# Two small opening loads change queue: c on GpSimd's, x tile 0 on SyncE's, in a kernel that keeps TensorE busy all the time

## The chip, the core and the metric

The kernel runs on one core of one Trainium2 chip. The metric is the device time of one execution in microseconds (us).

## The reference, cut to what matters

A vector c gives six modulation vectors. A block of layer norm, modulation and grouped-query attention follows (2048 queries and keys, 32 query heads on 8 key heads of width 128), then a gated MLP.

```python
mod = (_silu(c) @ w_mod).reshape(c.shape[0], 6, 1, -1)      # c: 1x512, w_mod: 512x3072
sa, ca, ga, sb, cb, gb = ...
h = _layernorm(x) * (1 + ca) + sa                             # x: 2048x512
x = x + ga * attention(h, k_cache, v_cache, wq, wo)
h = _layernorm(x) * (1 + cb) + sb
x = x + gb * gated_mlp(h, ...)
```

The first query projection needs `ca` and `sa`, which need silu(c) and the first two 512-column parts of `w_mod`. It also needs the first 128 rows of x (tile 0), normalised.

## The kernel before

Only the opening matters here: all loads that are wanted in the first 9 us, the work on c, and TensorE's program order up to the first attention scores. In these traces VectorE and the matmuls of TensorE keep the order in which the program emits them (in c_pool_warm_13_3, below, VectorE starts on a tile 3.6 us after it landed, because other work stood first), so this order is part of the argument.

```python
# loads. nc.scalar, nc.sync, nc.gpsimd name the engine whose queue takes the transfer
nc.scalar.dma_start(out=c_bf[:], in_=c_dram)                       # 1 KB
nc.scalar.dma_start(out=x_sb[:, 0, :], in_=x_dram[:, 0, :])         # tile 0, 128 KB
for i in range(2):
    part = slice(i * D, (i + 1) * D)
    nc.sync.dma_start(out=wmod_a[:, :, part], in_=wmod_dram[:, :, part])   # 512 KB each
# ... then on nc.sync: wq in two parts, k, x tile 1, k, x tiles 2 and 3, k transposed, v ...

# VectorE (nc.vector) and ScalarE (nc.scalar): silu of c
nc.vector.memset(zeros[:], 0.0)
nc.vector.memset(ones_bf[:], 1.0)
nc.vector.tensor_copy(out=c_f[:], in_=c_bf[:])
nc.scalar.activation(out=en[:], in_=c_f[:], func=ACT.Exp, scale=-1.0)
# ... on nc.vector: en + 1, sig = 1 / en, sc = c_f * sig
nc.vector.tensor_copy(out=sc_bf[:], in_=sc[:])

def warm(n):                       # n matmuls of zeros, 512 columns each
    ...

def mod_part(i, wmod, w0, mc_ps):  # 16 matmuls of one column
    for dt in range(NDT):
        for kt in range(NDT):
            nc.tensor.matmul(mc_ps[:, i * NDT + dt : i * NDT + dt + 1],
                lhsT=wmod[:, kt, w0 + dt * P : w0 + (dt + 1) * P],
                rhs=sc_bf[:, kt : kt + 1], ...)

# statistics of tile 0: bn_stats, bn_aggr on nc.vector, rstd on nc.gpsimd, normalise on nc.vector
xns0 = ln1_norm(0, 1, ln1_stats(0, 1))

warm(10)
mod_part(0, wmod_a, 0, mc_ps)      # wants part 0 of wmod_a, and sc_bf
warm(6)
mod_part(1, wmod_a, D, mc_ps)      # wants part 1
# ... four transposes of xn of tile 0, the query projection, the first scores (QK)
```

Of the kernel before, what the change touches and what calls it, by code (L numbers as in the profile page):

```python
# [575 lines left out]
def kernel(  # L576
# [19 lines left out]
    nc = tc.nc  # L596
# [21 lines left out]
    x_dram = A_x[0].rearrange("(t p) d -> p t d", p=P)  # L618
# [8 lines left out]
    c_dram = c[0].rearrange("(p j) -> p j", p=P)  # L627
# [19 lines left out]
    x_sb = res.tile([P, NT, D], BF16, name="x_sb")  # L647
# [46 lines left out]


    c_bf = res.tile([P, NDT], BF16, name="c_bf")
    nc.scalar.dma_start(out=c_bf[:], in_=c_dram)
    nc.scalar.dma_start(out=x_sb[:, 0, :], in_=x_dram[:, 0, :])
    for i in range(2):
        part = slice(i * D, (i + 1) * D)  # L700
        nc.sync.dma_start(out=wmod_a[:, :, part], in_=wmod_dram[:, :, part])
    k_nat = early.tile([P, SK], BF16, name="kT")

    def load_k_nat(half):
# [190 lines left out]
    for k in range(2):  # L895
        for dt in (2 * k, 2 * k + 1):
# [3 lines left out]
            else:  # L900
                nc.scalar.activation(
                    out=dst,
                    in_=src,
# [17 lines left out]
    for hf, copy in enumerate((nc.vector.tensor_copy, nc.scalar.copy)):  # L921
        copy(
            out=qTs[0][:, 2 * hf : 2 * hf + 2, 0:P],
            in_=q_ps[hf][:, 0 : 2 * P].rearrange("p (h q) -> p h q", h=2),
# [377 lines left out]
    for f in range(NFT):  # L1302
# [6 lines left out]
        out=ok1[:], in0=rall[:], scalar1=1.0 / SAFE, scalar2=None, op0=ALU.is_ge  # L1309
# [8 lines left out]
        out=bad[:], in0=okm[:], scalar1=-1.0, scalar2=1.0, op0=ALU.mult, op1=ALU.add  # L1318
# [137 lines left out]
```

## Time and profile before

| what | before | where from |
|---|---|---|
| time, median of six runs | 1321.10 us (1320.93 to 1321.20) | the runs |
| span of the profiled execution | 1319.7 us | the page |
| TensorE busy | 1312.4 us | the page |
| first modulation matmul | 5.42 us | timeline |
| second modulation, first matmul | 7.81 us | timeline |
| first scores (QK) matmul | 10.86 us | timeline |

TensorE does some 1300 us of matmuls with hardly a gap, so a delay of the first scores is a delay of the end.

From the view of the tile wmod_a in before, the time of its two transfers from issue to landing:

```profile
DMA to landing us min/median/max: 4.5/5.0/5.6
```

Six matmuls of zeros took 2.08 us; the cold rate, which the first ten show, is 0.43 us each, the warm rate 0.22 us. The landings: part 0 at 0.73 + 4.5 = 5.2 us, part 1 at 1.48 + 5.6 = 7.1 us.

### The profile page before, as it was taken

What the parts mean: (1) busy time and instruction counts of PE and PEld (TensorE: products, weight loads), DVE (VectorE), ACT (ScalarE), POOL (GpSimd) and SP (SyncE); (2) the same over time, 40 slices, a digit from 0 to 9 for tenths busy, and PEclk for the clock granted to TensorE, in tenths of its full rate; (3) what the DMA queues carried; (4) which work ended last, traced back from release to release, by engine and by line L of the source; (5) the groups of instructions that cost most, each with busy time, mean ns of one, the idle gap of its engine ahead of it and who ended that gap; (6) DMA issues with size and microseconds to landing.
All of it is one profiled execution on the core that took longest, in us unless ns stands there. A gap on an engine that the chain in (4) does not pass through costs nothing.

```text
span 1319.7 us, 27930 instructions
## 1 busy us (share of the span) xinstructions
PE 1312.4 (99%) x12359; PEld 858.6 (65%) x12359; DVE 470.7 (36%) x1162; ACT 1077.1 (82%) x1061; POOL 51.4 (4%) x96
## 2 busy tenths in 40 slices
PE   9999999999999999999999999999999999999998
PEld 5666666666666666666666666666666666644445
DVE  5622222222222222222222222222222566794444
ACT  7899999999999999999999999999999999650000
POOL 1201000000000000000000000000000000020000
PEclk9999999999999999999999999999999999999999
DMA  6542121112101111211110211121111112144300
GB/s 180 146 99 46 21 45 37 37 17 50 37 17 37 30 37 37 33 33 38 33 38 13 53 38 33 17 53 22 33 13 21 25 31 32 34 114 81 70 20 26
DMA packets 148944, 58.64 MB, mean 44 GB/s; under 512 B 138480, under 2 KB 144880, under 8 KB 148816
## 3 DMA queue, kind: packets, MB, share of 16 engines
q1 hardware_dynamic: 141792, 37.65, 15.4%
q0 software_dynamic: 4432, 16.91, 4.5%
q10 hardware_dynamic: 2592, 2.23, 0.5%
q8 instruction: 98, 1.61, 0.5%
q14 instruction: 30, 0.25, 0.1%
HBM read 21.89 MB, written 2.10 MB: 18 GB/s over the span
## 4 chain that ended last, share of the span: by engine, by line
PE 99%; DVE 0%; ACT 0%; issue 0%; DVEq 0%
PE o_ps L995 35%; PE s_ps L973 33%; PE misc L1027 8%; PE misc L940 8%; PE misc L1336 7%; PE s_ps L1182 2%; PE s_ps L1221 2%; PE o_ps L1357 1%; PE o_ps L781 1%; PE s_ps L1357 1%; PE misc L850 0%; DVE hT L809 0%; PE misc L1344 0%; ACT pT L980 0%; DVE tmp L1369 0%; DVE yout L1370 0%
## 5 line engine op out<-in xcount | busy, mean ns | idle before, releaser
L980 ACT ACTIVATE pT<-s_ps 128x1024 bf16<-128x1024 f32 x1024 | 1043.8, 1024 | 82.0 <-PE s_ps L973 6.7
L995 PEld LDWEIGHTS <-pT 128*128 128x128 bf16 x8192 | 548.5, 98 | 241.2
L995 PE MATMUL o_ps<-v,pT 128*128 128x129 bf16 x8192 | 631.5, 220 | 0.0
L973 PE MATMUL s_ps<-qT,kT 128*128 128x512 bf16 x2048 | 608.9, 379 | 0.3 <-ACT pT L980 0.2
L1006 DVE RECIPROCAL rall<-o_ps 128x2 f32<-128x2 f32 x256 | 43.5, 170 | 744.5 <-PE o_ps L995 741.1
L973 PEld LDWEIGHTS <-kT 128*128 128x128 bf16 x2048 | 199.3, 98 | 119.2 <-issue 0.8
L1027 PE MATMUL misc<-wo_g,oT 128*128 128x512 bf16 x512 | 194.1, 379 | 0.0
L940 PE MATMUL misc<-hT,wq_g 128*128 128x512 bf16 (+2 forms) x528 | 190.7, 371 | 0.1
L1007 DVE TENSOR_TENSOR onorm<-o_ps,rall 128x256 bf16<-128x256 f32 x256 | 108.6, 424 | 8.8
L1336 PE MATMUL misc<-wsp,z 128*128 128x512 bf16 (+2 forms) x560 | 100.7, 336 | 0.0
L951 DVE CAST qT<-misc 128x512 bf16<-128x512 f32 x127 | 86.2, 679 | 2.0 <-PE misc L940 2.0
L1336 PEld LDWEIGHTS <-z 128*128 128x128 bf16 x560 | 50.6, 98 | 48.5
L1040 DVE TENSOR_TENSOR xacc<-misc,xacc 128x512 f32<-128x512 f32 x112 | 76.0, 678 | 0.0
L940 PEld LDWEIGHTS <-wq_g 128*128 128x128 bf16 x528 | 50.4, 98 | 1.2 <-issue 0.4
L1027 PEld LDWEIGHTS <-oT 128*128 128x128 bf16 x512 | 50.1, 98 | 0.8
L1351 DVE TENSOR_TENSOR gb<-misc,bsp_bc 128x512 bf16<-128x512 f32 (+1 forms) x28 | 18.4, 658 | 58.9 <-PE misc L1336 58.9
L1182 PE MATMUL s_ps<-win_sb,hT 128*128 128x448 bf16 x128 | 27.0, 352 | 0.0
L1192 ACT ACTIVATE z<-s_ps 128x896 bf16<-128x896 f32 x16 | 14.7, 917 | 14.9 <-PE s_ps L1182 14.9
L1221 PE MATMUL s_ps<-hT,win_sb 128*128 128x512 bf16 x112 | 24.5, 379 | 0.0
L1229 ACT ACTIVATE z1T<-s_ps 128x1024 bf16<-128x1024 f32 x14 | 14.3, 1023 | 10.1 <-PE s_ps L1221 9.1
L692 DVE BATCH_NORM_STATS2 bnst<-x_sb 128x6 f32<-128x512 bf16 x32 | 21.8, 683 | 1.3 <-DMA x_sb<-in_A_x_dram 0.8
L1357 PE MATMUL o_ps<-wout_sb,yT 128*128 128x512 bf16 x84 | 20.1, 379 | 0.0
(88 smaller groups left out, 269.6 us busy)
## 6 DMA issues: line engine op xcount, KB each, us to landing
wq_g<-in_A_wq_dram POOLq DMA_DIRECT2D x7, 512.0 KB, 3.8
v<-in_A_v_cache_dram POOLq DMA_DIRECT2D x7, 512.0 KB, 6.0
wo_g<-in_A_wo_dram POOLq DMA_DIRECT2D x7, 512.0 KB, 4.7
oT<-onorm SPq DMA_TRANSPOSE x128, 2.4
wsp<-in_w_mod_dram POOLq DMA_DIRECT2D x1, 2048.0 KB, 9.0
out_dram<-yout ACTq DMA_DIRECT2D x16, 128.0 KB, 1.7
win_sb<-in_B_w_in_dram POOLq DMA_DIRECT2D x1, 1792.0 KB, 7.8
x_sb<-in_A_x_dram SPq DMA_DIRECT2D x3, 512.0 KB, 5.6
```

What stands on the lines that cost most here:

```text
L940: nc.tensor.matmul(ps[0][:, o0 : o0 + n], lhsT=wqs[g][:, dt, hh * DH : (hh + 1) * DH], rhs=hTs[ch][:, dt, c0 : c0 + n], start=(dt == 0), s ...
L951: nc.vector.tensor_copy(out=dst, in_=src)
L973: nc.tensor.matmul(s_ps[:, h * 512 : (h + 1) * 512].rearrange("p (r q) -> p r q", r=REP), lhsT=groups[g]["kT"][:, kt * P : (kt + 1) * P], ...
L980: nc.scalar.activation(out=pTs[u][:, 2 * i : 2 * i + 2, :], in_=s_ps[:].rearrange("p (k q) -> p k q", k=2), func=ACT.Exp, scale=inv_sqrt_dh,)
L995: nc.tensor.matmul(o_ps[:, hh % 2, 0 : DH + 1], lhsT=pTs[u][:, kt, hh * P : (hh + 1) * P], rhs=groups[g]["v1"][:, kt, 0 : DH + 1], start=( ...
L1007: nc.vector.tensor_tensor(out=onorms[u][:, hh - 1 : hh + 1, :], in0=o_ps[:, :, 0:DH], in1=rall[:, c0 : c0 + 2].unsqueeze(2).to_broadcast([ ...
L1027: nc.tensor.matmul(X_ps[:], lhsT=oTs[u][:, hh, :], rhs=groups[g]["wo"][:, hh, :], start=(hh == 0), stop=(hh == REP - 1),)
L1040: nc.vector.tensor_tensor(out=xaccs[j][:], in0=X_ps[:], in1=xaccs[j][:], op=ALU.add)
L1182: nc.tensor.matmul(ps[0][:, hf * 512 : hf * 512 + FC], lhsT=h2Ts[j // CT][:, dt, (j % CT) * P : (j % CT + 1) * P], rhs=win_sb[:, dt, FH + ...
L1221: nc.tensor.matmul(ps[0][:, k * 512 : (k + 1) * 512], lhsT=win_sb[:, dt, f * P : (f + 1) * P], rhs=h2Ts[2 * ch2 + k][:, dt, :], start=(dt ...
L1336: nc.tensor.matmul(g_ps[:, :n], lhsT=z2[:, st, f * P : (f + 1) * P], rhs=wsp[t][:, st, c0 : c0 + n], start=(st == 0), stop=(st == NT - 1 a ...
L1357: nc.tensor.matmul(dst, lhsT=yT[:, f, jj * P : (jj + 1) * P], rhs=wout_sb[:, f, :], start=(f == 0), stop=(f == NFT - 1),)
```

## The change

The intent is to free ScalarE's queue of loads, so that ScalarE starts its table load at once. c (1 KB) is to be read through GpSimd's queue, and tile 0 of x through SyncE's, between the two parts of the modulation weight.

```diff
     c_bf = res.tile([P, NDT], BF16, name="c_bf")
-    nc.scalar.dma_start(out=c_bf[:], in_=c_dram)
-    nc.scalar.dma_start(out=x_sb[:, 0, :], in_=x_dram[:, 0, :])
+    nc.gpsimd.dma_start(out=c_bf[:], in_=c_dram)
     for i in range(2):
         part = slice(i * D, (i + 1) * D)
         nc.sync.dma_start(out=wmod_a[:, :, part], in_=wmod_dram[:, :, part])
+        if i == 0:
+            nc.sync.dma_start(out=x_sb[:, 0, :], in_=x_dram[:, 0, :])
```

## The prediction

> **What bounds the kernel now.** I read the page's engine table first, then the chain that ended last, then the first 9 us of that chain, the waits of the first 24 us, and the timeline of the first 9 us, because the diff touches only transfers issued in the first 2.5 us. From the page, the line of busy times and the head of the chain:
>
> ```profile
> PE 1312.4 (99%) x12359; PEld 858.6 (65%) x12359; DVE 470.7 (36%) x1162; ACT 1077.1 (82%) x1061; POOL 51.4 (4%) x96
> ...
> PE 99%; DVE 0%; ACT 0%; issue 0%; DVEq 0%
> ```
>
> TensorE is busy for 1312.4 of 1319.7 us, and the chain runs through it for 99%. ScalarE (82%) and the DMA queues follow it. So only 7.3 us in the whole run is not TensorE work, and a change that touches no matmul can win only some of that, or lose by making TensorE wait. The start of the chain, in order of time (start us, us, what):
>
> ```profile
> 1.18 4.45 PE o_ps L781 x10
> 5.62 0.41 PE misc L850 x16
> 6.03 1.95 PE o_ps L781 x6
> 7.98 0.39 PE misc L850 x16
> ...
> 8.39 0.16 DVE modc L860
> ```
>
> L781 is not work: it is the warm-up, matmuls on zeros placed in TensorE's order so that the array is occupied while the first loads come in. L850 is the modulation, which needs the two parts of the modulation weight (wmod_a) and sc_bf, the silu of c. The chain goes from one to the other without a DMA, ScalarE or GpSimd in between: up to 8.39 us the path is the program order of TensorE. The loads that the change moves show up only as waits of other engines. In the waits of the first 24 us (engine, line, waited for: us in total, times, longest) these are the ones on c, x tile 0 and wmod_a:
>
> ```profile
> DVE c_f L766 <- DMA c_bf<-in_c_dram: 1.2, 1, 1.2
> ...
> DVE bnst L692 <- DMA x_sb<-in_A_x_dram: 0.8, 1, 0.8
> ...
> PEld L850 <- DMA wmod_a<-in_w_mod_dram: 0.5, 1, 0.5
> ```
>
> Whether each is hidden has to be read from the timeline of the first 9 us (start us, us, engine, line):
>
> ```profile
> 0.73 0.38 ACTq L697 DMA_DIRECT2D c_bf<-in_c_dram  x1
> ...
> 1.14 0.45 ACTq L698 DMA_DIRECT2D x_sb<-in_A_x_dram  x1
> ...
> 1.62 1.28 ACT L768 ACT_TABLE_LOAD   x1 [1.62 <-PEq L1440]
> ...
> 2.50 0.17 DVE L766 CAST c_f<-c_bf 128x4 f32<-128x4 bf16 x1 [1.24 <-DMA c_bf<-in_c_dram]
> ...
> 2.91 0.20 ACT L768 ACTIVATE en<-c_f 128x4 f32<-128x4 f32 x1
> ...
> 3.76 0.17 DVE L775 CAST sc_bf<-sc 128x4 bf16<-128x4 f32 x1
> ...
> 4.69 0.69 DVE L692 BATCH_NORM_STATS2 bnst<-x_sb 128x6 f32<-128x512 bf16 x1 [0.76 <-DMA x_sb<-in_A_x_dram]
> ...
> 5.24 0.70 PEld L850 LDWEIGHTS <-wmod_a 128*128 128x128 bf16 x16 [0.52 <-DMA wmod_a<-in_w_mod_dram]
> 5.42 0.61 PE L850 MATMUL misc<-sc_bf,wmod_a 128*128 128x1 bf16 x16
> ...
> 6.62 0.41 DVE L681 TENSOR_SCALAR xn<-x_sb,mv,rstd_ln 128x512 bf16<-128x512 bf16 x1 [1.02 <-POOL rstd_ln L677]
> ...
> 7.60 0.66 PEld L850 LDWEIGHTS <-wmod_a 128*128 128x128 bf16 x16
> ...
> 8.19 0.23 PEld L887 LDWEIGHTS <-xn 128*128 128x128 bf16 x4
> ```
>
> Four slacks follow. (a) c: sc_bf is done at 3.76 + 0.17 = 3.93, and its first use is at 5.42: slack 1.49 us. (b) x tile 0: xn is done at 6.62 + 0.41 = 7.03, TensorE turns to it at 8.19: slack 1.16 us. (c) Part 0 of wmod_a: the weight load waited until 5.24, but this was in the shadow of a warm-up matmul. The ten of L781 are 4.45 us long with the last one's drain, and the weight loads between them follow each other by 0.43 us, so number ten streams from 1.18 + 9 x 0.43 = 5.05 to about 5.45; the first modulation matmul starts at 5.42, just when the array is free. One weight load of up to 0.15 us fits into 5.24 to 5.42. So the 0.5 us wait costs at most 0.03 us. (d) Part 1: issued at about 1.44 and 5.6 us to landing (the longer of the two parts in that tile's view), so about 7.0, used at 7.60 with no wait recorded: slack 0.6 us.
>
> **What the Trainium skill says.** "DMA: Bandwidth & Descriptors", section "Issuing engines are not separate DMA queues": transfers issued from any engine run on the same 16 DMA engines and interleave, and another issuer saves only sequencer time. The trace agrees: x tile 0 on ACT's queue and part 0 on SyncE's share one stretch. By 4.25 us, ACT's queue had moved 283 of the 288 packets that it moves in all, and SyncE's 362 of the 528 that I count for part 0 (512 rows of 1 KB and one completion on each of 16 engines; the 288 are twice 128 + 16 in the same way). The same page, "Specifications", gives GpSimd's path a first-byte latency of about 1 us against 0.6 for SyncE's and ACT's. Here c on ACT's queue landed 1.8 us after its issue; GpSimd's own small transfer later (mod, 2 KB, issued at 105.22 and 0.76 us long) has its first packets at about 106.4, 1.2 us after issue, so the direction agrees. "ScalarE: Activation LUTs", section "What ACT_TABLE_LOAD costs", gives about 1283 ns for the load; the trace has 1.28 us. "TensorE: Matmul & The Clock Gate", Part 1, gives 426.7 ns from start to start for 512 columns on a cold array, which is the 0.43 us used in (c).
>
> **The change part by part.**
> ACT's queue loses two issues, 0.38 + 0.45 us with gaps: its table load moves from 1.62 to about 0.75 and ends near 2.03 instead of 2.90. Before, `en` at 2.91 was held by the table load, not by c_f (2.67). That is 0.2 us off the path to sc_bf, which has 1.49 us of slack: worth 0.
>
> c on GpSimd: issue at about 0.72 (where its first memset stands now), 0.76 us long, packets from 1.9 (1.2 us after issue). Its large weight loads (512 KB, 3.8 us to landing) leave 3.8 - 512/350 = 2.3 us when the bytes are taken at the 350 GB/s that the queue runs at from 4.25 us on. So I estimate a landing at 0.73 + 2.3 = 3.0, against 2.50 now. From there: c_f 0.17, step 0.05, en 0.20, and 0.82 from the end of en to the end of sc_bf (3.11 to 3.93), together 1.24: sc_bf at 4.25. Still 1.2 us before 5.42. GpSimd's memsets and the identity move by 0.76; the identity is done at about 2.1 and first used at 8.2. Worth 0.
>
> x tile 0 behind part 0 on SyncE's queue: SyncE's issue costs 0.45, after 0.70 for part 0, so at about 1.45. Its 128 KB now come after the 512 KB of part 0 instead of beside them. By 4.5 us both queues together had moved 0.46 + 0.13 MB; part 0 alone (0.52) would be through at about 4.35 instead of 4.7 and land near 4.85 instead of 5.24. x follows by 0.13/0.35 = 0.4 us and lands near 5.1 to 5.4 instead of 4.65. xn is then done at 7.03 + 0.45 to 0.75 = 7.5 to 7.8, before 8.19. Worth 0. Part 0 is 0.4 us earlier, worth at most the 0.03 of (c).
>
> The rest of SyncE's queue: each later issue is up to 0.45 us later, until x tiles 2 and 3. In the program before, that issue waits for a free completion semaphore, that of part 0 (issue at 5.21, after 4.86); the gap of 0.35 takes up most of the shift, so later ones go about 0.1 to 0.15 later. The queue is backlogged by then (DMA share 1.0 from 4 to 9 us, 331 to 376 GB/s), and the bytes ahead of part 1, wq and k are the same as before. Landings of these stay, within about 0.2 us, against the slack of 0.6 in (d).
>
> Sum: between -0.05 and 0 us. After 9 us nothing differs but this.
>
> **The rivals.** (1) c lands late on GpSimd's queue and TensorE waits for sc_bf. It needs a landing after 5.42 - 1.24 = 4.2, that is 3.5 us after issue. For it: mod took 11.1 us to landing. Against: that one writes DRAM, in 4-byte elements, and its 32 packets were through 1.8 us after issue. If c took 4.5 us, the start would slip by about 1 us: 1322.1. I give it 8%. (2) One queue feeds the DMA engines worse than two in the first 4 us, so part 1 comes more than 0.6 us late, or x more than 1.1 us late: +0.2 to +0.5 us, 1321.5. Against it: from 4.25 us on SyncE's queue alone holds 350 GB/s. 10%. (3) Part 0's earlier landing does shorten the start, if I read the modelled end of the warm-up wrongly: up to the 0.24 us between 5.00, where the weight load could have begun, and 5.24. 1320.9. 15%.
>
> **Range and chances.** The three runs of before span 0.26 us, and two builds may differ by some tenths. Predicted 1321.1, and 1320.5 to 1321.8 for 8 in 10; rival 1 is the tail above. Two per cent is 26 us, more than three times all time in which TensorE is idle, so faster 0.01; slower 0.01 for something unforeseen.
>
> **What would show it.** Right: table load at about 0.75; c_f near 3.0 and sc_bf below 5.0; weight load of L850 at 5.0 to 5.1 with the idle before it down to about 0.28; its first matmul still at 5.4; bnst of tile 0 at 5.1 to 5.4; second L850 still at about 7.6, and L887 at 8.2. Wrong: L850 waiting for sc_bf, L887 waiting for xn, or the first QK matmul (10.86 now) moved by more than 0.3 us.

## More of the kernel before

All 42 runs of the kernel before lie between 1320.58 and 1321.60 us, so the median of a few runs shows a difference of about half a microsecond.

The changed kernel has one line more, so L781, L850 and L887 of before are L782, L851 and L888 after.

From the timeline of before (start us, us, engine, line, what it writes and reads, how many), the second block of the warm-up:

```profile
5.89 2.08 PE L781 MATMUL o_ps<-onorm 128*128 128x512 bf16 x6
```

## The result, and the profile after

| | before | after |
|---|---|---|
| median of six runs | 1321.10 us | 1322.97 us |
| lowest to highest | 1320.93 to 1321.20 | 1321.84 to 1323.29 |
| span of the profiled execution | 1319.7 us | 1321.3 us |

A ratio here is the mean time of one kernel's fast runs over that of the other's of the same rounds, so it isn't quite the ratio of the medians. For this pair it is 1.0013, with an interval of 1.0000 to 1.0026. That is "the same" at 2%, as predicted. But the change costs 1.87 us by the medians, and 1322.97 lies above the predicted range of 1320.5 to 1321.8. None of the intervals in this document clearly excludes 1, so none shows a difference by itself. The argument rests on runs that don't overlap, as here (the fastest run of after, 1321.84, is slower than all 42 runs of before), and on the traces. The differences of 0.4 us for x0_pool and gap_sync, whose runs do overlap before's, are the weakest. The six runs of after fall apart, two at 1321.84 and 1322.23 and four from 1322.95 up; the profiled one, 1323.19, is of the upper four.

The page of after, the busy times and the head of the chain that ended last:

```profile
PE 1302.1 (99%) x12153; PEld 859.0 (65%) x12359; DVE 471.8 (36%) x1162; ACT 1077.1 (82%) x1061; POOL 52.4 (4%) x97
PE 98%; issue 1%; DVE 0%; DMA 0%; ACT 0%; POOLq 0%
```

TensorE's 1302.1 us isn't less work. The trace has 12153 matmul records against 12359 weight loads; before it had 12359 of both. The 206 missing records, not the change, make up the 10 us. What is new is that DMA and GpSimd's sequencer (POOLq) appear in the chain at all. The start of that chain in order of time (start us, us, what):

```profile
1.24 4.00 DMA c_bf<-in_c_dram
...
6.31 0.18 DVE sc_bf L776
6.50 0.04 issue
6.54 0.56 PE misc L851 x16
7.10 2.58 PE o_ps L782 x6
9.68 0.40 PE misc L851 x16
```

Before, this chain began, after the memset of the zeros, with ten warm-up matmuls of TensorE. Now it begins with a transfer: the load of c takes 4.00 us, and everything stands behind it. The timeline of after (columns as before; in brackets the idle time before it and what ended it) has the rest:

```profile
0.73 1.28 ACT L769 ACT_TABLE_LOAD   x1 [0.73 <-PEq L1441]
1.24 0.74 POOL L697 DMA_DIRECT2D c_bf<-in_c_dram  x1 [0.81 <-POOLq L1441]
5.00 0.15 PEld L851 LDWEIGHTS <-wmod_a 128*128 128x128 bf16 x1 [0.27 <-DMA wmod_a<-in_w_mod_dram]
5.26 0.17 DVE L767 CAST c_f<-c_bf 128x4 f32<-128x4 bf16 x1 [4.00 <-DMA c_bf<-in_c_dram]
6.39 0.69 DVE L692 BATCH_NORM_STATS2 bnst<-x_sb 128x6 f32<-128x512 bf16 x1
6.54 0.56 PE L851 MATMUL misc<-sc_bf,wmod_a 128*128 128x1 bf16 x16 [0.91 <-DVE sc_bf L776]
6.96 2.72 PE L782 MATMUL o_ps<-onorm 128*128 128x512 bf16 x6
12.60 0.59 PE L974 MATMUL s_ps<-qT,kT 128*128 128x512 bf16 x2
```

The table load did move to 0.73 as intended. It gains nothing, because the exponential now waits for c, not for the table. The weight for the modulation was in the array at 5.00, but its first matmul waited until 6.54 for sc_bf, and TensorE stood idle for 0.91 us. Then the second block of warm-up, which took 2.08 us before, took 2.72: all six ran at 0.43 us, so the clock rose later than it had before. The record of clock changes in the trace agrees: full speed begins at 10.31 us here, at 7.19 in before, and between 3.92 and 7.07 in the fourteen other profiles in which TensorE began at 1.18. The statistics of x tile 0 (bnst) began at 6.39 with no recorded wait for the tile: VectorE has them behind its work on c, and c was late.

Set side by side, in us from the start of the span:

| | before | after | shift |
|---|---|---|---|
| first modulation matmul | 5.42 | 6.54 | +1.12 |
| second modulation, first matmul | 7.81 | 9.48 | +1.67 |
| first scores matmul | 10.86 | 12.60 | +1.74 |
| span | 1319.7 | 1321.3 | +1.6 |

Of the shift, 1.12 is the wait for c, and 1.67 - 1.12 = 0.55 the slower warm-up. After that nothing more is lost. This reading is complete for this one execution, but it hides something. The view of wmod_a in after gives:

```profile
DMA to landing us min/median/max: 4.1/5.2/6.2
```

Part 1, issued at 2.13, landed at 2.13 + 6.2 = 8.3 us (8.37 by its completions, below), where before it had landed at about 7.1. TensorE came to it only at 9.05, so it waited for nothing here. Had c been early, it would have waited. There were thus two candidates, and the experiments had to separate them.

### The profile page after: what moved, and what is told of

Its sections match the earlier page's. It is cut to its first block, busy times and chain, and to the rows that moved or that the text cites. A ratio compares the mean times of both kernels' runs of the same rounds, so it can differ in the third digit from the quotient of the medians.

```text
span 1321.3 us, 27725 instructions
## 1 busy us (share of the span) xinstructions
PE 1302.1 (99%) x12153; PEld 859.0 (65%) x12359; DVE 471.8 (36%) x1162; ACT 1077.1 (82%) x1061; POOL 52.4 (4%) x97
## 4 chain that ended last, share of the span: by engine, by line
PE 98%; issue 1%; DVE 0%; DMA 0%; ACT 0%; POOLq 0%
PE s_ps L974 36%; PE o_ps L996 35%; PE misc L1337 7%; PE misc L941 7%; PE misc L1028 6%; PE s_ps L1183 2%; PE s_ps L1222 2%; PE o_ps L1358 1%; PE s_ps L1358 0%; DMA c_bf<-in_c_dram 0%; PE o_ps L782 0%; PE misc L851 0%; DVE hT L810 0%; PE misc L1345 0%; ACT pT L981 0%
## 5 line engine op out<-in xcount | busy, mean ns | idle before, releaser
L941 PE MATMUL misc<-hT,wq_g 128*128 128x512 bf16 (+2 forms) x465 | 167.3, 370 | 0.2
L1028 PE MATMUL misc<-wo_g,oT 128*128 128x512 bf16 x386 | 146.3, 379 | 0.0
L717 POOL DMA_DIRECT2D wq_g<-in_A_wq_dram x7 | 5.3, 751 | 370.5 <-PE misc L941 370.5
```

Source lines behind the costliest of these rows:

```text
L941: nc.tensor.matmul(ps[0][:, o0 : o0 + n], lhsT=wqs[g][:, dt, hh * DH : (hh + 1) * DH], rhs=hTs[ch][:, dt, c0 : c0 + n], start=(dt == 0), s ...
L1028: nc.tensor.matmul(X_ps[:], lhsT=oTs[u][:, hh, :], rhs=groups[g]["wo"][:, hh, :], start=(hh == 0), stop=(hh == REP - 1),)
```

## The experiments

The theory: c on GpSimd's queue comes late, TensorE waits for it, and the clock rises later because of that pause. The first rival: x tile 0 on SyncE's queue makes part 1 late, which would cost about as much if c didn't hide it. A second rival, for c itself: only GpSimd's late start delays it, not the traffic beside it. All kernels gave correct results. "Before" in each paragraph is the kernel before in the rounds on the same chip; its medians are 1321.18 us for c_pool_only, x0_sync_only, warm_13_3 and c_sync_first; 1320.94 for c_pool_warm_13_3, c_pool_quiet, before_again and part1_act; 1320.94 again for c_pool_stats_first, c_pool_alone, x0_pool and before_warm_10_4; and 1321.02 for x0_first_sync, x0_last_sync and gap_sync.

### One part of the change at a time

**c_pool_only**: c alone moves.

```diff
-    nc.scalar.dma_start(out=c_bf[:], in_=c_dram)
+    nc.gpsimd.dma_start(out=c_bf[:], in_=c_dram)
     nc.scalar.dma_start(out=x_sb[:, 0, :], in_=x_dram[:, 0, :])
```

> Only c moves to GpSimd's queue; x tile 0 stays on ACT's. Theory C (the whole loss is c: it lands near 5.2 instead of 2.5, TensorE waits 1.1 us for sc_bf, and because it stood idle its clock stays low through the second warm-up, another 0.6 us): as slow as the change, 1321.8 to 1323.3, c_f near 5.2, second warm-up block 2.7 us instead of 2.1. Rival X (the loss comes from x tile 0 and part 1 of the weight on one queue, part 1 landed near 8.3 instead of 7.0): 1321.1, as before.

Measured: five runs in two groups, 1321.81 and 1321.91 us with a mean granted clock of 1.000, and 1323.47, 1323.96 and 1324.13 us with 0.997 (ratio 1.0013, 0.9999 to 1.0027). So c alone costs 0.6 to 0.7 us, or 2.3 to 2.95 us; the upper group lies above what was expected. The profiled execution is one of the slow group. Its timeline, and two stretches of it (start:end in us, length, then busy time of TensorE, its weight loads, VectorE, ScalarE and GpSimd, each with a count, then the granted clock, the share of busy DMA engines, GB/s):

```profile
6.64 0.54 PE L850 MATMUL misc<-sc_bf,wmod_a 128*128 128x1 bf16 x16 [1.79 <-DVE sc_bf L775]
```

```profile
7.30:9.30 2.00, 2.00 (x6) 0.64 (x5) 0.51 (x2) 0.00 (x0) 0.81 (x2) 0.51 1.09 370
9.30:10.70 1.40, 1.40 (x22) 1.12 (x22) 0.64 (x4) 0.30 (x1) 0.00 (x0) 0.50 1.39 169
```

In this execution the clock had risen early, the ten warm-ups were done by 4.85, and TensorE idled 1.79 us. After that pause the granted clock was about half from 7.3 to 10.7 us. c landed at 5.34, as late as in the change, although x tile 0 was still on ScalarE's queue and had landed at 2.88. So c's lateness comes from its own move, and a pause of TensorE costs more than its own length. That the pause is what halves the clock isn't shown by this run alone; c_pool_warm_13_3 below takes only the pause away, and x0_last_sync compares the profiles that have one.

**x0_sync_only**: the other half, x tile 0 between the parts on SyncE's queue, c where it was before.

```diff
     nc.scalar.dma_start(out=c_bf[:], in_=c_dram)
-    nc.scalar.dma_start(out=x_sb[:, 0, :], in_=x_dram[:, 0, :])
     for i in range(2):
...
+        if i == 0:
+            nc.sync.dma_start(out=x_sb[:, 0, :], in_=x_dram[:, 0, :])
```

> c stays on ACT's queue, only x tile 0 moves to SyncE's between the two parts. Theory C: 1321.0 to 1321.3, sc_bf at 3.9, first modulation matmul at 5.42, tile 0's bnst at 5.0 to 5.5, QK at 10.86. Rival X: part 1 lands near 8.3 again, the second modulation's weight load waits for it 0.7 us, 1321.7 to 1322.0.

Measured: 1322.31 us (1321.87 to 1322.42), ratio 1.0008 (0.9994 to 1.0022), 1.1 us above before. c was early (sc_bf done at 3.72), and TensorE waited for part 1 instead. Its timeline:

```profile
7.92 0.55 PE L851 MATMUL misc<-sc_bf,wmod_a 128*128 128x1 bf16 x16 [0.52 <-DMA wmod_a<-in_w_mod_dram]
```

The rival is real: with the same bytes ahead of it, part 1 landed at 7.88 us, 0.8 later than before. The time is somewhat above the 1321.7 to 1322.0 expected for it. The two halves cost 0.6 to 2.95 and 1.1 us alone, and 1.87 together. They don't simply add, because each lateness hides part of the other. By the medians c alone (2.3) even costs more than the whole change: three of its five runs have the clock of 0.997, which none of the change's six have.

### Hiding one of the two

**warm_13_3**: the changed kernel with three warm-up matmuls moved from the second block to the first, so that TensorE has work until c comes.

```diff
-    warm(10)
+    warm(13)
     mod_part(0, wmod_a, 0, mc_ps)
-    warm(6)
+    warm(3)
```

> The change with 13 and 3 warm-up matmuls instead of 10 and 6, so that TensorE does not stand idle until sc_bf, and does the same number of them. Theory C: sc_bf still near 6.4, first modulation near 6.7, no idle time, the clock rises where it did before (near 7.3); if part 1 has landed by 7.6, 1321.0 to 1321.4, if it lands at 8.3, 1321.6 to 1322. If the loss were the transfer itself and not TensorE's idle time and cold clock: 1322 to 1323 as with the change.

Measured: 1322.16 us (1322.01 to 1322.42), ratio 1.0008 (0.9994 to 1.0021). sc_bf was done at 6.41, nearly as late as in the change (6.48), but the first modulation started at 6.70 with no idle time before it. The three warm-ups then took 0.81 us, so the clock had risen. Next in the timeline stands a wait for part 1, which landed at 8.19:

```profile
8.23 0.55 PE L851 MATMUL misc<-sc_bf,wmod_a 128*128 128x1 bf16 x16 [0.30 <-DMA wmod_a<-in_w_mod_dram]
```

With the pause taken away, the median falls by 1322.97 - 1322.16 = 0.81 us, and the runs spread over 0.41 us instead of the change's 1.45. What is left, 1322.16 - 1321.18 = 0.98 us, is about what x0_sync_only lost to part 1. But it isn't part 1's alone, since the normalised x of tile 0 (xn) was ready only at 8.66, its statistics having stood behind the work on the late c:

```profile
8.25 0.41 DVE L681 TENSOR_SCALAR xn<-x_sb,mv,rstd_ln 128x512 bf16<-128x512 bf16 x1 [1.02 <-POOL rstd_ln L677]
```

The transposes of xn started at 8.72, just after the second modulation. With part 1 on time they would still have waited until about then. So some 0.8 us of the change's 1.87 is the pause with its effect on the clock. The other 1 us has two causes that end together, part 1 and the statistics behind the late c, and this run doesn't separate them. The median is above the 1321.6 to 1322 that was expected for a late part 1, and at the low end of what was expected if the pause didn't matter (1322 to 1323). What speaks against the latter is the timeline, without idle time and with the clock up.

**c_pool_warm_13_3**: the same shift of warm-ups, in c_pool_only.

```diff
-    nc.scalar.dma_start(out=c_bf[:], in_=c_dram)
+    nc.gpsimd.dma_start(out=c_bf[:], in_=c_dram)
...
-    warm(10)
+    warm(13)
     mod_part(0, wmod_a, 0, mc_ps)
-    warm(6)
+    warm(3)
```

> c alone on GpSimd's queue, x tile 0 on ACT's, with 13 and 3 warm-up matmuls. Theory C2 (two separate costs: c's lateness with the idle time and the cold clock behind it, which the moved warm-up hides, and x tile 0 in SyncE's queue, which is not here): 1321.1 to 1321.6, and no second mode near 1324. If c on GpSimd's queue by itself also makes part 1 late (7.8 in the profile of c_pool_only): 1321.9 to 1322.4.

Measured: 1322.14 us (1321.89 to 1322.24), ratio 1.0009 (0.9995 to 1.0022). The slow group of c_pool_only is gone in all five runs, and no clock of 0.997 is seen. That fits the pause as the cause of the halved clock. But the time missed the expectation of theory C2 on the high side. Part 1 did land late, at 7.54, as the other branch has it, but its weight load waited only 0.17 us for it. What TensorE waited for is in the timeline:

```profile
6.48 0.69 DVE L692 BATCH_NORM_STATS2 bnst<-x_sb 128x6 f32<-128x512 bf16 x1
8.88 0.23 PE L887 MATMUL misc<-ident,xn 128*128 128x128 bf16 x1 [0.59 <-DVE xn L681]
```

x tile 0 had landed at 2.86 us, and its statistics still began at 6.48, straight after the last step on c. The work on c stands first in VectorE's program order. A late c thus delays the normalised x as well, and TensorE waits for that at 8.88.

**c_pool_stats_first**: c_pool_warm_13_3, with the statistics and the normalisation of tile 0 emitted before the work on c.

```diff
     nc.vector.memset(ones_bf[:], 1.0)
...  # tiles st0 and xn0
+    nc.vector.bn_stats(out=st0[:, 0, :], in_=x_sb[:, 0, :])
+    nc.vector.bn_aggr(out=mv1[:, 0, :], in_=st0[:])
+    rstd0 = rstd_of(mv1[:, 0:1, :], 1, "ln1")
+    normalise(xn0[:], x_sb[:, 0, :], mv1[:, 0, 0:1], rstd0[:, 0:1])
     nc.vector.tensor_copy(out=c_f[:], in_=c_bf[:])
...
-    xns0 = ln1_norm(0, 1, ln1_stats(0, 1))
+    xns0 = [xn0]
```

> c_pool_warm_13_3 with the statistics and the normalisation of x tile 0 ahead of c's chain in VectorE's order. If what is left of c's cost there (1.2 us) is VectorE's order (bnst at 6.48 although tile 0 had landed at 2.9, then TensorE waiting 0.6 us for xn): bnst at 2.9, L887-type transposes right after the second modulation, and 1321.1 to 1321.6. If it is part 1 of the weight or anything else: 1322.0 to 1322.3 again.

Measured: 1321.71 us (1321.56 to 1322.14), ratio 1.0006 (0.9993 to 1.0020). That is 0.4 us less than c_pool_warm_13_3, slightly above what was expected, and still 0.77 above before. The transposes of x follow the second modulation without a wait now. What remains is c, in the timeline:

```profile
6.94 0.54 PE L856 MATMUL misc<-sc_bf,wmod_a 128*128 128x1 bf16 x16 [1.32 <-DVE sc_bf L781]
```

In this execution the clock rose early, the thirteen warm-ups had run out by about 5.6, and c landed at 5.64.

### Why c is late

**c_sync_first**: the changed kernel with c at the head of SyncE's queue.

```diff
-    nc.gpsimd.dma_start(out=c_bf[:], in_=c_dram)
+    nc.sync.dma_start(out=c_bf[:], in_=c_dram)
```

> c as the first load of SyncE's queue, x tile 0 between the two parts: ACT's queue holds no load either, but GpSimd none too. Theory C (it is GpSimd's path that is slow): c lands near 2.5, 1321.0 to 1321.4. If c is slow wherever it meets part 0 of the weight in the DMA engines: c lands after 4, and 1322 to 1323. Rival X: 1321.7 to 1322.

Measured: 1322.74 us (1322.33 to 1323.99), ratio 1.0013 (1.0000 to 1.0027). c landed at 2.50 as in before, so GpSimd's queue is what makes it late. But the time hardly fell. The issue of c pushes the others back by 0.4 us (part 1 issued at 2.56), part 1 landed at 8.93, and TensorE waited for it:

```profile
8.98 0.55 PE L851 MATMUL misc<-sc_bf,wmod_a 128*128 128x1 bf16 x16 [1.73 <-DMA wmod_a<-in_w_mod_dram]
```

An early c doesn't pay as long as part 1 is late: a second sign that both parts of the change cost. The time is above what rival X expected (1321.7 to 1322), as part 1 came later still than in the change. The slowest of the five runs, 1323.99, is the only one with a clock of 0.997. This kernel too has a long pause of TensorE (1.73 us), as c_pool_only has, though in the profiled run (0.999) no halved clock follows it.

**c_pool_quiet** (a single look): c on GpSimd's queue, VectorE's two opening memsets moved to GpSimd behind it, and a second load of c, to a tile c_q, later when the queues are quiet.

```diff
-    nc.scalar.dma_start(out=c_bf[:], in_=c_dram)
+    nc.gpsimd.dma_start(out=c_bf[:], in_=c_dram)
...
-    nc.vector.memset(zeros[:], 0.0)
-    nc.vector.memset(ones_bf[:], 1.0)
+    nc.gpsimd.memset(zeros[:], 0.0)
+    nc.gpsimd.memset(ones_bf[:], 1.0)
...  # in the fourth call of rstd_of:
+    nc.gpsimd.dma_start(out=c_q[:], in_=c_dram)
+    nc.gpsimd.tensor_copy(out=c_q2[:], in_=c_q[:])
```

> Measures GpSimd's load of c by itself: the load at the start without any VectorE memset before it (GpSimd does them afterwards, so TensorE starts near 2.9 and the time is some 2 us longer, which is not the point), and the same load of c once more near 23 us, when the DMA engines are idle. If GpSimd's issue at 1.24 instead of 0.72 was held up by VectorE's memsets: it now starts at 0.75. If it is a start-up of its own: 1.24 again. If the 4.0 us to landing are SyncE's packets ahead of it: near 2 us in the quiet stretch. If they are the path itself: 3.5 to 4 in both.

Measured: 1323.25 us in its one run, which isn't the point, since the zeros came late and TensorE began at 3.29. The timeline of the opening, and the view of the tile c_q:

```profile
1.24 0.74 POOL L705 DMA_DIRECT2D c_bf<-in_c_dram  x1 [0.81 <-POOLq L1448]
```

```profile
DMA to landing us min/median/max: 2.0/2.0/2.0
```

Two things follow. GpSimd's issue starts at 1.24 again, where its first memset stood at 0.72 in before, and it does so with no memset of VectorE beside it: the late start is GpSimd's own. Nor can work of VectorE be what holds c's transfer, since VectorE's first instruction there starts at 5.53, when c has landed. And the same load takes 2.0 us from issue to landing in a quiet stretch, against 4.3 at the start of the same execution.

**c_pool_alone** (a single look): the changed kernel, with a small copy of c at the head of SyncE's queue, which holds all other loads back until c has landed.

```diff
     nc.gpsimd.dma_start(out=c_bf[:], in_=c_dram)
+    c_go = res.tile([P, NDT], BF16, name="c_go")
+    nc.sync.dma_start(out=c_go[:], in_=c_bf[:])
```

> The change, but SyncE's queue waits for c before its first load (a tiny copy of c), so that GpSimd's load of c runs with no other load in the DMA engines. If c's 4.0 us come from part 0 of the weight ahead of it in the DMA engines: first packet about 1.4 us after the issue, landing 2.0 to 2.3 us after it, near 3.4. If they are a start-up of GpSimd's first load: landing near 5.2 again. The whole time is some us longer, which is not the point.

Measured: 1325.64 us in its one run; all loads are late by design. With nothing beside it, c landed about 2.1 us after its issue, in the timeline:

```profile
3.39 0.17 DVE L769 CAST c_f<-c_bf 128x4 f32<-128x4 bf16 x1 [2.12 <-DMA c_bf<-in_c_dram]
```

So the 4.0 us of the change are 2.1 us of this path alone and 1.9 us that SyncE's loads beside it cost, part 0 of the weight first of all. The trace agrees: in the change, c's first packet moved at 3.81 us, and the 528th packet of SyncE's queue, the last of part 0 by count, at 4.06. The second rival for c falls: of c's 2.76 us of delay (5.24 against 2.48), the late start is 0.5, the longer path about 0.4 (2.12 against 1.75), and the traffic 1.9. In the seven profiles with a load on GpSimd's queue beside SyncE's, its first packet moved at 3.81 to 3.99 us; why it waits so long is not shown.

### Why part 1 is late

**before_again** (a single look): the kernel before, unchanged, as a second profile.

```diff
(no edit)
```

> The kernel before once more, for a second profile. Theory S (part 1 of the weight and the loads after it land about 1 us later in every variant because of where x tile 0 and c stand): part 1 lands at 7.0 to 7.2, as in the first profile, few packets stalled. Rival R (single packets stall at random for 0.3 to 1.4 us, in the kernel before too, and the first profile was a lucky one): part 1 lands anywhere from 7.0 to 7.9. Time 1321.0 to 1321.5 in both.

Measured: 1321.02 us, span 1319.2. In this execution the second block of warm-up took 1.46 us instead of 2.08, since the clock had risen earlier, and in the timeline the second modulation waits for its weight:

```profile
5.85 1.46 PE L781 MATMUL o_ps<-onorm 128*128 128x512 bf16 x6
7.20 0.47 PEld L850 LDWEIGHTS <-wmod_a 128*128 128x128 bf16 x16 [0.38 <-DMA wmod_a<-in_w_mod_dram]
```

Most of these 0.38 us lie behind the warm-up, whose last matmul streams until about 5.85 + 6 x 0.22 = 7.2. Part 1 landed at 7.16, about as in the first profile (7.08). So the slack of 0.6 us that the first profile shows for it is a matter of when the clock rises. In other executions there is none.

**part1_act**: c and part 1 on ScalarE's queue, part 0 and then x tile 0 on SyncE's.

```diff
-    nc.scalar.dma_start(out=x_sb[:, 0, :], in_=x_dram[:, 0, :])
     for i in range(2):
...
-        nc.sync.dma_start(out=wmod_a[:, :, part], in_=wmod_dram[:, :, part])
+        (nc.sync, nc.scalar)[i].dma_start(out=wmod_a[:, :, part], in_=wmod_dram[:, :, part])
+        if i == 0:
+            nc.sync.dma_start(out=x_sb[:, 0, :], in_=x_dram[:, 0, :])
```

> c on ACT's queue and after it part 1 of the weight too; SyncE's queue holds part 0, then x tile 0. The same bytes in two rings. If it is the single ring that makes part 1 late: part 1 lands by 7.1, second modulation at 7.6 without a wait, 1321.0 to 1321.4. If it is x tile 0 behind part 0, or chance, part 1 still lands at 7.7 or later and the time is 1321.9 to 1322.4, as in x0_sync_only.

Measured: 1322.20 us (1321.99 to 1322.42), ratio 1.0010 (0.9996 to 1.0024), which misses the expectation. Part 1 did come early, at 6.82. But x tile 0 landed only at 6.51 (5.66 in the change), its statistics began at 6.54, and the loss moved there, in the timeline:

```profile
6.86 0.47 PEld L851 LDWEIGHTS <-wmod_a 128*128 128x128 bf16 x16 [0.45 <-DMA wmod_a<-in_w_mod_dram]
8.94 0.23 PE L888 MATMUL misc<-ident,xn 128*128 128x128 bf16 x1 [1.53 <-DVE xn L681]
```

**x0_pool**: the kernel before with x tile 0 on GpSimd's queue, c as before.

```diff
-    nc.scalar.dma_start(out=x_sb[:, 0, :], in_=x_dram[:, 0, :])
+    nc.gpsimd.dma_start(out=x_sb[:, 0, :], in_=x_dram[:, 0, :])
```

> c on ACT's queue as before, x tile 0 on GpSimd's. SyncE's queue is as in the kernel before. If part 1 is late because it shares one queue with x tile 0 and is issued 0.7 us later: part 1 lands at 7.0 to 7.3. Tile 0 itself should land at 5 to 6 (as c did from that queue); if below 5.8, 1321.0 to 1321.5, if later, TensorE waits for xn by the difference. If part 1 is late whatever queue takes x: 7.7 or later and 1322.2.

Measured: 1321.38 us (1321.29 to 1321.64), ratio 1.0004 (0.9990 to 1.0017). x tile 0 landed at 5.44, as late as in x0_sync_only (5.45), but part 1 at 6.88. The time is 0.44 us above its before, against 1.13 for x0_sync_only, and the first scores start at 10.80, between before's profile (10.86) and before_again's (10.37). So a tile 0 at 5.44 costs about 0.4 us here. With tile 0 off SyncE's queue but still beside part 0, part 1 isn't late.

**x0_first_sync** and **x0_last_sync** (the second a single look): x tile 0 on SyncE's queue, ahead of both parts or behind both, c as before.

```diff
-    nc.scalar.dma_start(out=x_sb[:, 0, :], in_=x_dram[:, 0, :])
+    nc.sync.dma_start(out=x_sb[:, 0, :], in_=x_dram[:, 0, :])      # x0_first_sync
     for i in range(2):
...
+        if i == 1:                                                  # x0_last_sync
+            nc.sync.dma_start(out=x_sb[:, 0, :], in_=x_dram[:, 0, :])
```

> c on ACT's queue, SyncE's queue holds x tile 0, part 0, part 1. If standing between the parts is what makes part 1 late: part 1 lands near 7.1, part 0 about 0.4 us later than in x0_sync_only (5.5), 1321.1 to 1321.4. If it is one queue for all bytes, or the later issue (2.1): part 1 at 7.7 or later, the 16 engines spread over 1.5 us or more, 1321.9 to 1322.5.

> SyncE's queue holds part 0, part 1, x tile 0: one queue, but part 1 issued at 1.44 as before and with 0.13 MB less ahead of it. If one queue by itself spreads the engines: part 1's 16 engines land over 1.5 us or more, the last after 7.3. If it is the later issue or x tile 0 ahead of it: spread under 0.9 us, landing at 6.3 to 6.8. Tile 0 then comes late (near 7) and TensorE waits for xn, so the time is some 1 to 1.5 us longer, which is not the point.

Measured: x0_first_sync 1321.95 us (1321.54 to 1323.46), ratio 1.0011 (0.9997 to 1.0024); part 0 landed at 6.25 and part 1 at 7.68. x0_last_sync 1324.37 us in its one run; part 0 landed at 5.65, part 1 at 7.03 although 128 KB fewer were ahead of it, and x at 7.39, for which TensorE waited at 9.81. Spreads of about 1.2 us (below) fit neither branch of the two expectations. No place in SyncE's queue is free of cost.

But the 1324.37 isn't the price of the place alone. After the wait of 1.69 us for x, the record of clock changes has half speed from 9.88 to 13.29. Six profiles have a pause of over 1 us after the clock's first rise. In c_pool_only (1.79), x0_last_sync (1.69) and c_pool_alone (3.06) half speed followed; in c_pool_stats_first (1.32), part1_act (1.53) and c_sync_first (1.73) it didn't. So the length of the pause alone doesn't decide.

In all three that halved, half speed began 3.41 us after the rise and lasted 3.41 us. One may therefore cut the time into pieces of 3.41 us, forward and backward from the rise. In the three that halved, one piece held 1.69 to 3.0 us of idle time of TensorE; in the other three no piece held more than 1.32, since in c_sync_first and part1_act the end of a piece divides the pause. The rise fits too: in all 17 profiles the piece just before it held 0.68 us of idle time or less, and the one before that 0.81 or more. In the change the latter, from 3.49 to 6.90, holds the pause of 0.91 us. This is a pattern in 17 profiles, and no run tests it.

**gap_sync**: the kernel before, with a 1 KB load between the two parts on SyncE's queue, so that part 1 is issued at 2.13 as in the change, but x tile 0 stays on ScalarE's.

```diff
         nc.sync.dma_start(out=wmod_a[:, :, part], in_=wmod_dram[:, :, part])
+        if i == 0:
+            c_gap = res.tile([P, NDT], BF16, name="c_gap")
+            nc.sync.dma_start(out=c_gap[:], in_=c_dram)
```

> As before, with a tiny load (c once more, into a tile that nobody reads) between the two parts on SyncE's queue, so that part 1 is issued 0.4 to 0.5 us later; x tile 0 stays on ACT's queue. If the later issue makes part 1 late: 7.5 or later, spread over 1.2 us, 1321.6 to 1322.2. If x tile 0 in SyncE's queue does: part 1 at 7.0 to 7.3, 1321.0 to 1321.3.

Measured: 1321.43 us (1321.17 to 1322.88), ratio 1.0006 (0.9993 to 1.0020). From the view of the tile wmod_a:

```profile
DMA to landing us min/median/max: 4.5/4.7/4.9
```

Part 1 was issued at 2.13 and landed at 2.13 + 4.9 = 7.0, as in before. By this profile, which is of the fastest of the five runs, a later issue isn't the cause of the lateness. The time is still 0.4 above before and misses the 1321.0 to 1321.3 expected. In the trace TensorE's weight loads wait 0.24 us for wq at 8.27 and 0.37 for k at 9.42, which they don't in before: the loads behind the parts do come later. x0_sync_only has both waits too (0.2 and 0.3), so not all of its 1.1 us is part 1.

A transfer here reports one completion from each of 16 DMA engines, and it has landed when the last has. The trace has these completions one by one. In the table, "spread" is the time from the first of part 1's 16 to the last; the last column says what else was in transit.

| kernel | part 1 landed (us) | spread (us) | beside the parts |
|---|---|---|---|
| before, twice | 7.08, 7.16 | 0.76, 0.74 | x tile 0 on ScalarE's queue |
| before_warm_10_4 | 6.88 | 0.49 | the same |
| gap_sync | 7.00 | 0.60 | the same |
| x0_pool | 6.88 | 0.69 | x tile 0 on GpSimd's queue |
| part1_act | 6.82 | 0.75 | part 1 itself on a second queue |
| after | 8.37 | 2.04 | x tile 0 on SyncE's, between the parts |
| x0_sync_only | 7.88 | 1.73 | the same |
| warm_13_3 | 8.19 | 2.13 | the same |
| c_sync_first | 8.93 | 2.54 | the same, c ahead |
| x0_first_sync, x0_last_sync | 7.68, 7.03 | 1.18, 1.24 | x tile 0 on SyncE's, first or last |
| c_pool_only | 7.79 | 1.91 | x tile 0 on ScalarE's, landed at 2.88 |
| c_pool_warm_13_3, c_pool_stats_first | 7.54, 7.49 | 1.62, 1.53 | the same, at 2.86 and 2.83 |
| c_pool_quiet | 6.78 | 0.83 | the same, at 2.83 |

(c_pool_alone, whose loads all start later, has 11.96 and a spread of 2.18.) Where tile 0 or part 1 was on another queue through the time of part 0, the 16 completions stay within 0.8 us. Where tile 0 was in SyncE's queue with both parts, they spread over 1.2 to 2.5 us. But with c on GpSimd's queue and tile 0 early from ScalarE's they spread over 1.5 to 1.9 us in three of four profiles. So the move of c alone goes with a late part 1 as well, and SyncE's queue holding tile 0 isn't the whole condition. The middle engine of the 16 is as early in x0_sync_only (6.58) as in before (6.57); only the slow ones are late. In after the middle is at 7.3, so there the whole transfer is later too. Single packets of 1 KB take 0.2 to 1.4 us on single engines, in before as well (0.61 at most up to 9 us), so stalls are no mark of the change; their number and place differ. Why packets stall, and why a second queue beside the first keeps the engines together, stays open. It is a correlation over one profile of each kernel. c_pool_quiet, with the same opening transfers as c_pool_only and a spread of 0.83 against 1.91, shows that chance is in it.

### Is there something to gain?

**before_warm_10_4**: the kernel before with two warm-up matmuls fewer in the second block.

```diff
-    warm(6)
+    warm(4)
```

> The kernel before with 4 instead of 6 warm-up matmuls in the second block. If the second block, and not the landing of part 1 (7.1 to 7.2), sets the second modulation in most runs: 0.2 to 0.4 us faster than before, 1320.6 to 1320.9. If part 1 sets it in most runs (as in before_again, where TensorE waited 0.38 us for it): the same time within 0.1 us.

Measured: 1320.99 us (1320.60 to 1321.28), ratio 1.0000 (0.9987 to 1.0014). In its profile, the weight of the second modulation waits for part 1 (landed at 6.88) until 6.92, when the four warm-ups have just ended, so shorter filler gains nothing. None of the kernels beat the kernel before.

## Why the prediction was right or wrong

**Right: the bound and the class.** A change that touches no matmul moved the time by 0.14% (1.87 of 1321.10), far within 2%.

**Right: the gains are worth nothing.** The table load moved to 0.73 and was worth 0. Part 0 arrived about 0.4 us earlier, its weight load stood at 5.00 with the idle before it at 0.27, both as written, and was worth 0.

**Wrong: c on GpSimd.** The step that failed is "I estimate a landing at 0.73 + 2.3 = 3.0". It landed at 1.24 + 4.00 = 5.24. The issue was put where a memset had stood, which is 0.5 us too early. The 1.2 us from issue to first packet, read from mod, was also short: the trace has mod's first packet at 106.61, 1.4 us after its issue. The 2.3 us were worked out from a transfer that had the queues nearly to itself. As a figure for a quiet path they are good: 2.0 and 2.1 us were measured. But this load runs beside 512 KB of another queue, and c_pool_alone shows that SyncE's loads added 1.9 us. The prediction had itself shown that this stretch was full of part 0's packets, and didn't ask what they do to c's. The rest of that step follows: c_f at 5.26 instead of 3.0, sc_bf at 6.48 instead of 4.25, and 1.06 us too late for a matmul at 5.42.

Rival 1 of the prediction is what happened, with its 8%. Its size, 1 us and 1322.1, was right for the wait alone. It left out two things that a late c does: TensorE's pause makes the clock rise later (0.55 us in after's profile) or fall to half (c_pool_only's slow group), and VectorE's program order holds the statistics of tile 0 behind c.

**Wrong: x tile 0.** The statistics were predicted at 5.1 to 5.4 and began at 6.39. The completions put the tile's landing at 5.66, so the landing was only 0.3 us off; what held the statistics was VectorE's order. In x0_sync_only, where c is early, they begin at 5.47. That the later tile by itself is worth 0 holds only roughly: x0_pool, with the tile at 5.44, is 0.4 us above before.

**Wrong: part 1.** The step is "Landings of these stay, within about 0.2 us, against the slack of 0.6 in (d)". Both halves failed. The landing moved from 7.08 to 8.37 in the change and to 7.88 in x0_sync_only. The bytes ahead in the queue, which were the same, didn't determine when the slowest of the 16 engines was done. And the slack, 0.5 rather than 0.6 us by the completions, was read from one execution in which the clock had risen late; before_again has none. Rival 2 of the prediction named this (more than 0.6 us late) and gave it 10%, but at +0.2 to +0.5 us. x0_sync_only lost 1.1. The rival's mechanism, one queue that feeds the engines worse than two, isn't shown.

**The range.** It was built from the spread of before's runs, as if the two steps above were certain. The sum in place of "between -0.05 and 0": about 0.8 us for TensorE's pause and the clock, and about 1 us for part 1 and for the statistics behind the late c, which end together, against 1.87 measured. The two terms come from taking the pause away (warm_13_3) and from what then remained. The cause of part 1's spread is open.

## What to carry to other kernels

A tiny load is not a cheap load when the first work of the busiest engine waits for it: judge its landing in the traffic that it will meet, and not from the same queue at a quiet time. A slack read from one execution of a start-up phase is only as good as that execution, since the clock's rise moves the consumer by half a microsecond or more from run to run; profile it twice. After moving a load, also ask what stands behind its first reader in that engine's program order. And before the rest of a loss is put down to the wait that is seen, look at what would have ended just as late without it.

## What the Trainium skill lacked or had wrong

- "DMA: Bandwidth & Descriptors", section "Specifications", gives a first-byte latency of about 1 us for GpSimd's path. In c_pool_alone and c_pool_quiet, with nothing or little beside it, the first packet of a 1 KB load came 1.4 to 1.5 us after the start of its issue and the landing 2.0 to 2.1 us after it. Beside a 512 KB transfer on another queue they were 2.6 (3.81 - 1.24) and 4.0 us after. That section has no figure for a load that meets such traffic.
- The same page, section "Queues, rings and completion order", says that each DMA engine takes turns between queues packet by packet, a packet being typically 9 to 17 descriptors and at most 64. For x tile 0 on ScalarE's queue beside part 0, before agrees. For c on GpSimd's queue no taking turns shows: the first of its packets moved at 3.81 us, when part 0 was nearly through (its last at 4.06, by count). The trace lists single pieces of 1 KB and doesn't show the page's packets, so this isn't a contradiction.
- The same page, section "Issuing engines are not separate DMA queues", has all issuers on the same 16 DMA engines, and the page's rules say that spreading transfers over issuers only saves issue time. Here part 1's completions spread over 1.2 to 2.5 us with tile 0 and both parts in one queue, and over 0.5 to 0.8 us with bulk on a second queue beside part 0, part 1 landing at 7.0 to 8.9 or at 6.8 to 7.2. The cause isn't shown.
- "TensorE: Matmul & The Clock Gate", Part 1, has the clock fall after an idle window of about 3.4 us. In c_pool_only a pause of 1.79 us was followed by half the clock for 3.4 us (7.3 to 10.7), in x0_last_sync one of 1.69 us (9.88 to 13.29), so a wholly idle window wasn't needed. The page's remark that the window runs freely and so differs between runs agrees: 2.08 against 1.46 us for the same six matmuls in two executions of before.
- No page that I found says that GpSimd's first transfer starts later than another first instruction of it would: it is recorded at 1.24 us, where its memset had started at 0.72 (after, c_pool_only, c_pool_quiet, x0_pool).
